# Storing the last group's output as two half tiles from two queues, in a fused attention and gated feed-forward kernel

## The chip, the cores and the metric

The kernel runs on one core of a Trainium2 chip. The core has a matrix engine (TensorE, PE in the rows; its weight loads are PEld), a vector engine (VectorE, DVE), an activation engine (ScalarE, ACT), GpSimd (POOL) and SyncE (SP), which here does nothing but issue transfers and wait. Transfers are carried by 16 DMA engines that all issuing engines share; each issuer has a queue of its own, in the rows q1 for SyncE, q10 for ScalarE and q0 for GpSimd. The metric is the device time of one execution in microseconds (us). The times are medians of several executions.

## The reference

Two branches read the same x of 2048 tokens by 512: attention with 32 heads of size 16 that share one k and one v, and a GeGLU feed-forward layer of width 1376. A sigmoid gate for each token mixes them. All is float32.

```python
def _A_ref(x, wq, wk, wv, wo):
    q = (x @ wq).reshape(B, S, H, Dh).transpose(0, 2, 1, 3)
    k = x @ wk
    v = x @ wv
    scores = einsum("bhqd,bkd->bhqk", q, k) * (Dh ** -0.5)
    o = einsum("bhqk,bkd->bhqd", softmax(scores), v)
    return o.transpose(0, 2, 1, 3).reshape(B, S, H * Dh) @ wo

def _B_ref(x, w_gate, w_up, w_down):
    return (gelu(x @ w_gate) * (x @ w_up)) @ w_down

g = sigmoid((x * gate_w).sum(-1, keepdims=True))
return g * _A_ref(...) + (1 - g) * _B_ref(...)
```

## The kernel before

The 2048 tokens are four groups of 512 (`NTG`, `TG`). The operands of the projections and of the feed-forward layer are split in a high and a low half, and each product is done in three passes. After a prologue, a table of lines (`PLAN`) sets the order on TensorE by hand: each line plays one job of the feed-forward layer (`f`) or of the output projection (`w`), with score matmuls and value matmuls of the attention put between its pieces.

For each group an accumulator `acc[g]` of 128 x 4 x 512 in SBUF holds four row tiles of 128 tokens. The feed-forward jobs add to it, weighted by one minus the gate (line 617). Then, for each row tile i, the output projection's matmuls leave a bank in PSUM, and `wo_out` (lines 625 to 628) adds that bank, times the gate, to the row tile with one VectorE instruction (line 627) and stores the finished 128 x 512 tile, 256 KB, to `out` with one transfer that SyncE issues (line 628).

Groups 0 to 2 reach `wo_out` through jobs of the table, in the middle of the stream. The last group, 3, is done behind the table (lines 882 to 889): twelve chains of matmuls first sum up three quarters of the projection for all four row tiles, while VectorE finishes the last heads' normalisation (lines 776 to 794); then, row tile by row tile, three matmuls end the chain (line 501) and `wo_out` follows. No other work comes after it. ScalarE's last work is the last exponential of the scores (line 749).

Each engine runs its own instructions in the order in which they are written, and semaphores tie them to each other. Transfers issued by SyncE or ScalarE count on eight semaphores, DMAHW0 to DMAHW7, which the transfers of the whole program take in turn. At the end of the program (rows of line 928) SyncE waits for all of them, in the order of their numbers and each in an instruction of its own, before all engines meet and the program is over.

Of the kernel before, what the change touches and what calls it, by code (L numbers as in the profile page):

```python
# [19 lines left out]
P = 128  # L20
# [5 lines left out]
TG = 512  # L26
NTG = S // TG
# [84 lines left out]
def mix_kernel(ctx, tc, xT, wq, wo, wf, out):  # L112
    nc = tc.nc
# [511 lines left out]
    def wo_out(g, i, ps):  # L625
        o = acc[g][:, i]
        nc.vector.scalar_tensor_tensor(o, ps, gt[:, 4 * g + i : 4 * g + i + 1], o, op0=ALU.mult, op1=ALU.add)  # L627
        nc.sync.dma_start(out[g * TG + i * P : g * TG + (i + 1) * P], o)

    def wo_job(g, i):  # L630
        def begin():
            assert ("o", 0, NB - 1) in done
            flush(bg)
            return [[t for bl in range(NB) for t in wo_terms(g, k, bl)] for k in (i, i + 1)]

        def end(z, y):
            wo_out(g, i, z)
            wo_out(g, i + 1, y)

        return begin, end  # L640
# [44 lines left out]
    with tc.If(v > 0):  # L685
        with tc.tile_pool(name="gp", bufs=1) as gp:
# [4 lines left out]
            with tc.For_i(0, NTG * NB, 1) as gb:  # L691
                with tc.For_i(0, 2, 1) as a:
                    t = gp.tile([P, 2, TG], F32R, tag="gq", name="gq", bufs=2)
                    rows = scr[bass.ds(gb, 1)].rearrange("o r (a h) q -> (o r) a h q", a=2)
# [187 lines left out]
    g = NTG - 1  # L882
# [4 lines left out]
    for i, ps in enumerate(tail):  # L887
        chain_mm(ps, wo_terms(g, i, NB - 1), first=False)
        wo_out(g, i, ps)
# [42 lines left out]
```

## Time and profile before

| what | us |
|---|---|
| median of 3 runs | 1230.28 |
| range of the runs | 1230.28 to 1230.36 |
| the profiled execution, its own time | 1231.25 |
| its span, first to last instruction | 1229.5 |
| TensorE busy in the span | 1222.6 |
| ScalarE busy in the span | 1029.4 |
| VectorE busy in the span | 546.1 |

The profile is one execution, taken by the hardware's profiler. A row of the timeline has the start in us from the span's start, the length, the engine, the line of the kernel, the operation, what it writes and reads, and how many instructions the row merges. An engine's name with a q behind it is its sequencer, which waits, branches and issues transfers: a row "SPq ... DMA_DIRECT2D" is the time in which SyncE issues, not the time in which the bytes move. When they move is told by the DMA view and by the windows, whose last two columns are the mean busy share of the 16 DMA engines and the GB/s that they moved. A share a little over 1 arises where a packet that began in a window ends after it.

### The profile page before, as it was taken

The page shows a single profiled execution, that of the slowest core. Times are in us where ns is not written, and L with a number is a line of the kernel's source. Part 1 is how long each engine was busy: PE and PEld are TensorE (multiplying, and loading weights), DVE is VectorE, ACT ScalarE, POOL GpSimd, SP SyncE. Part 2 cuts the span into 40 slices and gives each one's busy share as a digit, 9 for nine tenths or more (in the row PEclk, how much of TensorE's full clock was granted, in tenths as well). Part 3 has the DMA queues.
Part 4 walks back from the last instruction along what each step waited for, and adds up shares of the span by engine and source line. Part 5 has one row for each costly group of instructions (what it writes and reads, how often), then busy time and mean ns, then how long its engine had stood idle before and what let it go on. Part 6 is the DMA issues. An engine that isn't in the chain of part 4 may idle for free.

```text
span 1229.5 us, 23232 instructions
## 1 busy us (share of the span) xinstructions
PE 1222.6 (99%) x9742; PEld 671.4 (55%) x9742; DVE 546.1 (44%) x812; ACT 1029.4 (84%) x1127; POOL 216.9 (18%) x188
## 2 busy tenths in 40 slices
PE   9999999999999999999999999999999999999998
PEld 6875455555554555455555555654554555545545
DVE  7774422656245151545436152263626244044624
ACT  5549888888888888998888888889888898889983
POOL 5422201222121010212112020121311011012100
PEclk9999999999999999999999999999999999999999
DMA  8641202212021110122211120111211211002000
GB/s 333 211 135 52 72 1 58 66 53 79 27 68 51 44 32 23 49 57 67 66 35 58 39 76 15 42 44 56 83 41 49 75 49 32 23 27 66 15 1 35
DMA packets 39835, 73.88 MB, mean 60 GB/s; under 512 B 5488, under 2 KB 5744, under 8 KB 39728
## 3 DMA queue, kind: packets, MB, share of 16 engines
q1 hardware_dynamic: 39184, 71.32, 18.9%
q8 instruction: 77, 1.26, 0.4%
q0 software_dynamic: 256, 0.79, 0.2%
q14 instruction: 30, 0.25, 0.1%
q10 hardware_dynamic: 288, 0.26, 0.1%
HBM read 57.41 MB, written 14.94 MB: 59 GB/s over the span
## 4 chain that ended last, share of the span: by engine, by line
PE 93%; DVE 0%; ACT 0%; issue 0%
PE acc L816 38%; PE s L745 23%; PE z L515 21%; PE y L515 10%; PE wos L501 1%; PE u L501 0%; DVE acc L627 0%; ACT p L749 0%; PE wof L501 0%; DVE sq L545 0%; DVE sq L544 0%; DVE gs L541 0%; ACT sq L548 0%
## 5 line engine op out<-in xcount | busy, mean ns | idle before, releaser
L749 ACT ACTIVATE p<-s 128x1024 f32<-128x1024 f32 x1024 | 976.3, 1026 | 139.1 <-PE s L745 136.2
L816 PE MATMUL acc<-p,v 128*32 128x512 f32 x4096 | 484.8, 597 | 0.0
L745 PE MATMUL s<-Q,kp 51*128 51x512 f32 x2048 | 384.8, 415 | 0.1
L745 PEld LDWEIGHTS s<-Q,kp 51*128 51x128 f32 x2048 | 184.2, 184 | 214.1 <-ACT p L749 124.0
L816 PEld LDWEIGHTS acc<-p,v 128*32 128x32 f32 x4096 | 114.3, 109 | 250.8 <-issue 242.1
L187 POOL TENSOR_TENSOR gl<-st,gh 128x512 fp32r<-128x512 f32 x80 | 114.0, 1444 | 754.3 <-PE s L745 375.5
L515 PE MATMUL z<-xh,gh 64*128 64x512 f32 x312 | 125.9, 403 | 0.0
L515 PE MATMUL y<-xh,gh 64*128 64x512 f32 x312 | 125.8, 403 | 0.0
L515 PE MATMUL y<-xl,gh 64*128 64x512 f32 x312 | 122.4, 392 | 0.0
L515 PE MATMUL z<-xl,gh 64*128 64x512 f32 x312 | 122.1, 391 | 0.0
L515 PE MATMUL z<-xh,gl 64*128 64x512 f32 x312 | 121.8, 390 | 0.0
L515 PE MATMUL y<-xh,gl 64*128 64x512 f32 x312 | 121.7, 390 | 0.0
L541 DVE COPY gs<-z 128x512 f32<-128x512 f32 x39 | 27.0, 692 | 195.3 <-PE y L515 128.5
L187 POOL TENSOR_TENSOR dl<-st,dh 128x512 fp32r<-128x512 f32 x44 | 57.3, 1304 | 127.8 <-PE s L745 94.0
L515 PE MATMUL z<-dh,hh 64*128 64x512 f32 x176 | 69.5, 395 | 0.0
L515 PE MATMUL y<-dh,hh 64*128 64x512 f32 x176 | 69.5, 395 | 0.0
L515 PE MATMUL y<-dl,hh 64*128 64x512 f32 x176 | 68.9, 392 | 0.0
L515 PE MATMUL z<-dl,hh 64*128 64x512 f32 x176 | 68.8, 391 | 0.0
L515 PE MATMUL z<-dh,hl 64*128 64x512 f32 x176 | 68.8, 391 | 0.0
L515 PE MATMUL y<-dh,hl 64*128 64x512 f32 x176 | 68.7, 391 | 0.0
L515 PEld LDWEIGHTS z<-xh,gh 64*128 64x128 f32 x312 | 58.0, 186 | 15.6 <-POOLq L523 7.3
L515 PEld LDWEIGHTS z<-xl,gh 64*128 64x128 f32 x312 | 58.3, 187 | 8.2
(173 smaller groups left out, 1458.0 us busy)
## 6 DMA issues: line engine op xcount, KB each, us to landing
st<-wf SPq DMA_DIRECT2D x125, 256.0 KB
scr<-q SPq DMA_DIRECT2D x16, 512.0 KB
Q<-scr SPq DMA_DIRECT2D x64, 128.0 KB
Q<-scr SPq DMA_DIRECT2D x64, 64.0 KB
out<-acc SPq DMA_DIRECT2D x16, 256.0 KB
xr<-xT SPq DMA_DIRECT2D x6, 512.0 KB
st<-xT SPq DMA_DIRECT2D x12, 256.0 KB
xr<-xT SPq DMA_DIRECT2D x4, 256.0 KB
```

The costliest lines, as they stand in the source:

```text
L187: eng_l.tensor_sub(lo, src, hi)
L501: nc.tensor.matmul(ps, a, b, start=(first and q == 0), stop=(last and q == len(terms) - 1), skip_group_check=True)
L515: mm = nc.tensor.matmul(ps, a[rs], b[rs], start=(half == 0 and q == 0), stop=(half == 1 and q == len(X) - 1), skip_group_check=True)
L541: nc.vector.tensor_copy(gs, g)
L745: nc.tensor.matmul(ps[:, j * TG : (j + 1) * TG], kp[rs, kc * P : (kc + 1) * P], Q[u][rs, pr], start=True, stop=True)
L749: nc.scalar.activation(pb[s][:, pr], ps, AF.Exp, bias=0.0, scale=SCALE)
L816: nc.tensor.matmul(accp[u][32 * j : 32 * j + 32], vt[:, kc], pb[s][:, j // 2, (j % 2) * TG : (j % 2 + 1) * TG], start=(kc == 0), stop=(kc ...
```

## The change

`wo_out` keeps its VectorE instruction. For groups 0 to 2 the store is as before. For the last group each store is written as two: rows 0 to 63 of the tile from SyncE, rows 64 to 127 from ScalarE. Each half is 128 KB.

```diff
     def wo_out(g, i, ps):
         o = acc[g][:, i]
         nc.vector.scalar_tensor_tensor(o, ps, gt[:, 4 * g + i : 4 * g + i + 1], o, op0=ALU.mult, op1=ALU.add)
-        nc.sync.dma_start(out[g * TG + i * P : g * TG + (i + 1) * P], o)
+        rows = out[g * TG + i * P : g * TG + (i + 1) * P]
+        if g < NTG - 1:
+            nc.sync.dma_start(rows, o)
+        else:
+            nc.sync.dma_start(rows[0 : P // 2], o[0 : P // 2])
+            nc.scalar.dma_start(rows[P // 2 : P], o[P // 2 : P])
```

The last instructions of SyncE before the change, from the last loads of the attention's queries (`Q`) on; `acc` is the accumulator of the last group, and behind "waits" stand the semaphores that an instruction waits for:

```order
L368 DMA Q_12177<-scr 16x2x512
L373 DMA Q_12177<-shs 3x2x512 [waits DMAHW2_49]
L373 DMA Q_12177<-shs 3x2x512 [waits DMAHW3_49]
L628 DMA out<-acc_11092 128x512 [waits DMAHW4_49,DVE_49]
L628 DMA out<-acc_11092 128x512 [waits DMAHW5_49,DVE_49]
L628 DMA out<-acc_11092 128x512 [waits DMAHW6_49,DVE_49]
L628 DMA out<-acc_11092 128x512 [waits DMAHW7_49,DVE_49]
L928 UNCONDITIONAL_BRANCH
```

Each store takes the next semaphore; it waits until the earlier transfer that counted on the same semaphore is over, and for VectorE. The same place after the change, on SyncE:

```order
L368 DMA Q_12177<-scr 16x2x512
L373 DMA Q_12177<-shs 3x2x512 [waits DMAHW2_49]
L373 DMA Q_12177<-shs 3x2x512 [waits DMAHW3_49]
L632 DMA out<-acc_11092 64x512 [waits DMAHW5_49,DVE_49]
L632 DMA out<-acc_11092 64x512 [waits DMAHW7_49,DVE_49]
L632 DMA out<-acc_11092 64x512 [waits DMAHW1_49,DVE_49]
L632 DMA out<-acc_11092 64x512 [waits DMAHW3_49,DVE_49]
L933 UNCONDITIONAL_BRANCH
```

and at the end of ScalarE, where before the change the branch followed the last exponential:

```order
L754 ACTIVATE p<-s 128x1024 [waits PE_49]
L633 DMA out<-acc_11092 64x512 [waits DMAHW4_49,DVE_49]
L633 DMA out<-acc_11092 64x512 [waits DMAHW6_49,DVE_49]
L633 DMA out<-acc_11092 64x512 [waits DMAHW0_49,DVE_49]
L633 DMA out<-acc_11092 64x512 [waits DMAHW2_49,DVE_49]
L933 UNCONDITIONAL_BRANCH
```

SyncE still issues four times, each for half the rows; ScalarE has four issues more; and the last pair of stores counts on DMAHW2 and DMAHW3, where the last store counted on DMAHW7. The order on the other engines is the same.

## The prediction

> **What bounds the kernel now.** I read the page first, then the chain of waits over the end of the span, then the timeline and the DMA view of that end, because the change touches nothing before it. The page:
>
> ```profile
> span 1229.5 us, 23232 instructions
> PE 1222.6 (99%) x9742; PEld 671.4 (55%) x9742; DVE 546.1 (44%) x812; ACT 1029.4 (84%) x1127; POOL 216.9 (18%) x188
> ```
>
> TensorE is busy in 99% of the span, so the time is TensorE's stream plus what follows its last matmul. The stores of groups 0 to 2 lie under that stream and are not changed. The chain of waits, from 1222 us on (start, length, what), the timeline there, and TensorE's, VectorE's and SyncE's rows:
>
> ```profile
> 1222.20 0.69 PE wos L501 x3
> 1222.90 0.02 issue
> 1222.92 2.79 DVE acc L627 x4
> ...
> 1210.79 1.03 ACT L749 ACTIVATE p<-s 128x1024 f32<-128x1024 f32 x1
> ...
> 1224.53 0.39 PE L501 MATMUL wof<-woh,ol 128*128 128x512 f32 x1
> 1224.96 0.75 DVE L627 SCALAR_TENSOR_TENSOR acc<-wof,gt,acc 128x512 f32<-128x512 f32 x1
> ...
> 1223.70 2.37 SPq L628 DMA_DIRECT2D out<-acc  x4
> ```
>
> The chain ends with four additions of VectorE, each worth about 0.7 us, the last over at 1222.92 + 2.79 = 1225.71. SyncE issues one store behind each of them, from 1223.70 to 1226.07. ScalarE's last exponential is over at 1211.82, so ScalarE is idle here. From 1225.71 to the end of the span, 1229.5, there is no arithmetic: 3.8 us of stores and closing. That is the whole stage this change can act on. The DMA engines in it, by windows (columns: stretch, length, busy time of PE, PEld, DVE, ACT, POOL, clock, DMA share, GB/s):
>
> ```profile
> 1223.60:1224.50 0.90, 0.90 (x5) 0.75 (x4) 0.90 (x3) 0.00 (x0) 0.00 (x0) 1.00 0.00 0
> 1224.57:1227.46 2.90, 0.35 (x2) 0.00 (x0) 1.14 (x2) 0.00 (x0) 0.00 (x0) 1.00 0.96 362
> 1224.57:1225.25 0.68, 0.35 (x2) 0.00 (x0) 0.68 (x2) 0.00 (x0) 0.00 (x0) 1.00 0.98 364
> 1225.25:1227.30 2.05, 0.00 (x0) 0.00 (x0) 0.46 (x1) 0.00 (x0) 0.00 (x0) 1.00 1.02 384
> 1227.46:1229.49 2.03, 0.00 (x0) 0.00 (x0) 0.00 (x0) 0.00 (x0) 0.00 (x0) 0.55 0.02 4
> ```
>
> Nothing moves for 0.87 us after the first issue (1223.70 to 1224.57). Then the 16 engines are full until 1227.46, at 362 GB/s: four stores of 256 KB are 1.05 MB, and 1.05 / 0.362 = 2.9 us. The stores come one each 0.68 us and one takes 0.256 / 0.38 = 0.68 us to move, so the engines never run dry and never fall far behind. Two things therefore set the end of the transfers at the same place: the first byte plus 2.9 us of bytes (1227.46), and the last store by itself, which if it met empty engines would end at 1225.74 + 0.87 + 0.68 = 1227.3. Behind the bytes SyncE's own waits are the last to end:
>
> ```profile
> SPq L928 <- DMA out<-acc: 1.2, 2, 0.6
> ...
> L928 SPq EVENT_SEMAPHORE  x8: 17/28/28, 1226.1 to 1226.5; - x8
> ...
> L928 SPq EVENT_SEMAPHORE  x2: 28/28/28, 1227.2 to 1227.8; - x2
> L928 SPq DRAIN  x1: 7/7/7, 1227.9 to 1227.9; - x1
> ```
>
> The ten closing waits of SyncE are in these rows: the first eight find their semaphores ready and start 0.4 / 7 = 0.06 us apart; the ninth runs at 1227.2 and the tenth at 1227.8, each held back by a store. The tenth waits for the last store, and runs 0.36 us after the last byte. Then come a drain and the meeting of all engines, to 1229.5.
>
> **The change, part by part.**
>
> *Issue.* Four stores of 128 rows on SyncE become four of 64 rows there and four of 64 rows on ScalarE. What is queued behind them: on SyncE only the closing waits, on ScalarE only its closing branch. One issue costs, by the rows of SyncE over the whole kernel (ns, least / median / most):
>
> ```profile
> L628 SPq DMA_DIRECT2D out<-acc x16: 332/353/375, 407.1 to 1225.7; - x16
> ...
> L367 SPq DMA_DIRECT2D Q<-scr x64: 312/414/1487, 70.6 to 1140.7; - x64
> L368 SPq DMA_DIRECT2D Q<-scr x64: 414/425/1307, 71.1 to 1141.2; - x64
> ```
>
> Line 628 issues 128 runs of 2 KB, line 367 issues 64, line 368 issues 32. Fewer runs are not cheaper: 0.35, 0.41, 0.43 us. So a half costs SyncE 0.33 to 0.43 us, ends before the next store is due 0.68 us later, and I take 0 change. Nor does the delay to the first byte hang on the size. A lone 64-run load and a lone 128-run load:
>
> ```profile
> 1139.89 0.33 SPq L367 DMA_DIRECT2D Q<-scr  x1
> ...
> 1139.80:1140.80 1.00, 1.00 (x14) 0.33 (x12) 0.96 (x2) 0.90 (x1) 0.00 (x0) 1.00 0.00 0
> 1140.80:1140.90 0.10, 0.10 (x8) 0.03 (x2) 0.10 (x1) 0.10 (x2) 0.00 (x0) 1.00 0.91 123
> ...
> 1131.57 0.33 SPq L349 DMA_DIRECT2D st<-wf  x1
> ...
> 1131.50:1132.50 1.00, 1.00 (x12) 0.83 (x10) 0.00 (x0) 1.00 (x2) 0.04 (x1) 1.00 0.00 0
> 1132.50:1132.60 0.10, 0.10 (x4) 0.08 (x2) 0.00 (x0) 0.10 (x1) 0.00 (x0) 1.00 0.49 123
> ```
>
> Both start to move between 0.91 and 1.03 us after their issue. So SyncE's first half should move at 1224.57, as now. For ScalarE's half the only row is the program's start, where both queues issue at once:
>
> ```profile
> 0.76 0.40 ACTq L166 DMA_DIRECT2D st<-wf  x1
> ...
> 0.77 1.83 SPq L169 DMA_DIRECT2D xr<-xT  x4
> ...
> q1 hardware_dynamic: 8, 0.02, 13.4%
> ...
> q1 hardware_dynamic: 33, 0.07, 71.8%
> q10 hardware_dynamic: 33, 0.02, 16.3%
> ```
>
> The third row is the DMA view of 1.80 to 2.25 us, where only SyncE's queue (q1) moves; the last two are 2.25 to 2.60 us, where ScalarE's (q10) has joined. Issued together, ScalarE's first byte came about 0.44 us after SyncE's. The delay of ScalarE's half is so bounded by 0.87 and 0.87 + 0.44 us. At the first it costs nothing. At the second, ScalarE's first half moves at 1225.01 while SyncE's 128 KB last until 1224.57 + 0.34 = 1224.91: the engines lose 0.1 us once. I take the nearer end, 0, and keep 0.1 for the range.
>
> *Bytes.* The same 1.05 MB move on the same 16 engines, with 16 more of the smallest packets for each of the four added transfers:
>
> ```profile
> DMA packets 576, 1.05 MB, mean 328 GB/s; under 512 B 64, under 2 KB 64, under 8 KB 576
> ```
>
> Of 576 packets 64 are under 512 B, 16 a store; now they will be 128. Were one as long as a mean packet (0.96 x 2.90 x 16 / 576 = 0.077 us), the added four on each engine would cost 0.31 us. But the stretch that holds nearly all of them ran at 384 GB/s and the stretch that holds none at 364, so they cost next to nothing: I take 0.03, with 0 and 0.31 for the range.
>
> [...]
>
> *The closing waits.* Each transfer counts on the next of eight semaphores in turn, and SyncE closes by waiting for them by number, DMAHW0 to DMAHW7. The order of instructions shown ahead has the last stores before on DMAHW4 to 7, so the last to land was the last waited for. After the change they run over 4, 5, 6, 7, 0, 1, 2, 3, and the last pair, 2 and 3, lands while SyncE has five or four more waits to walk. At 0.06 us each, that is 0.24 to 0.3 us which lie under the transfers now and will lie behind the last byte. I take 0.3. It would be 0 if the waits' cost ran beside the 0.36 us that a landing takes to be seen, and that is the lower end.
>
> *Sum.* Issue 0, bytes 0.03, closing waits 0.3: +0.33 us. The profiled execution has 1231.25 us, 1229.5 of span and 1.75 around it, so its like after the change has 1231.6 with a span of 1229.8. The median of the plain runs is 1230.28, 0.97 below that execution; the same step on it gives 1230.6.
>
> **The rivals.** First, *the issue hardware serves the two queues in turn*. For it speaks the 0.44 us at the start; against it that SyncE's issues there were no longer than alone. If every half took 0.44 us, the eighth would begin at 1224.57 + 7 x 0.44 = 1227.65 and end 0.34 later, at 1227.99: 0.53 us late, and with the closing waits 1230.28 + 0.53 + 0.3 = 1231.1.
>
> Second, *two queues fill the engines better*. For it a row of the busiest stretch, 20.0 to 20.5 us, where two queues share the engines:
>
> ```profile
> DMA packets 86, 0.21 MB, mean 426 GB/s; under 512 B 15, under 2 KB 15, under 8 KB 86
> ...
> q0 software_dynamic: 39, 0.11, 56.9%
> q1 hardware_dynamic: 47, 0.10, 50.6%
> ```
>
> At 426 GB/s the last store still begins at 1225.74 + 0.87 and ends 0.6 later, 1227.21: a gain of 0.25 against +0.3 of waits, 1230.2. Against it: the engines are already full at a share of 1.02. Were the waits free besides, it would be 1230.0, and that is the best case I can build. A gain of 0.2% would have to end the transfers before VectorE's last addition.
>
> Third, on the other side, *half the rows, half the rate*: 64 rows can be read only half as fast, and both queues' packets come in step, so that the engines ask first for the upper rows and then for the lower. At half of 362 GB/s the transfers take 5.8 us instead of 2.9; with the waits 1230.28 + 2.9 + 0.3 = 1233.5, 0.26% slower. It decides from a mean rate under about 210 GB/s (2.9 + 2.16 us), where the 2.46 us of 0.2% are reached. Against it is the same row: q0 there is GpSimd's store of 32 rows (786 KB in all from a zeroed tile),
>
> ```profile
> shs<-woh POOLq DMA_DIRECT2D x4, 192.0 KB, 7.1
> ```
>
> and it moved 0.11 MB in 0.5 us, 220 GB/s, beside another queue's 0.10 MB, with the engines' total at 426. A quarter of the rows did not slow the engines, so two interleaved halves should not.
>
> That the change does not do what it says can be excluded on the issue side: the order of instructions has the four halves on ScalarE, behind its last exponential, with nothing else there.
>
> **How the numbers follow.** Forecast 74%; served in turn 10%; better filled 8%; half the rate 6%; and 2% for shifts that I cannot name. About 0.2%, 2.46 us, is what a measurement of this kernel can tell from no change. Only the third rival passes it: slower 6%, faster 1%, the same 93%. The predicted time is the forecast's, 1230.6. The range takes in the first two rivals and the added bounds (0.1 for ScalarE's delay, 0.31 for small packets): 1230.1 to 1231.4; below and above it lie the half-rate case and the far ends, less than 2 in 10.
>
> **What would show it.** Right: q1 and q10 with about 0.52 MB each in the last 5 us, together at 360 to 390 GB/s from 1224.6 to 1227.5; four ACTq issues of 0.33 to 0.47 us from 1223.7 on; four or five closing waits of SyncE 0.06 us apart after 1227.5, and a span longer by 0.3. Wrong: q10's first byte more than 0.5 us behind q1's, gaps in the DMA row, a rate near 200 GB/s, or a closing that follows the last byte as fast as now. Any change of TensorE's stream before 1222 us would also make the sum wrong, since I give it none.

## The result and the profile after

| | before | after |
|---|---|---|
| median of 14 executions, us | 1230.32 | 1232.66 |
| lowest and highest, us | 1229.93, 1231.39 | 1232.02, 1233.41 |
| profiled execution: time, span, us | 1231.25, 1229.5 | 1233.26, 1231.5 |

The ratio after to before is 1.0017, with a 95% interval of [1.0009, 1.0025]: 2.1 us longer, between 1.1 and 3.1 (the two medians are 2.3 apart). The forecast was 0.33 us longer, 1230.6, and the stated range ended at 1231.4. Executions of one kernel differ by over a microsecond, and the profiles differ by as much in their first 80 us, far ahead of the edited stores: the first exponential starts at 81.3 us in the profile of before, at 81.5 after, at 79.6 and 79.9 in two of the runs below. So the parts are measured here from the end of VectorE's last addition, behind which only the stores and the closing lie. Before, that tail lasts from 1225.71 to 1229.49: 3.78 us.

The timeline after the change, VectorE's and the two issuing queues' rows (start, length, engine, line, operation):

```profile
1223.22 2.11 DVE L627 SCALAR_TENSOR_TENSOR acc<-wos,gt,acc 128x512 f32<-128x512 f32 x3 [0.58 <-PE wos L501]
1225.26 0.75 DVE L627 SCALAR_TENSOR_TENSOR acc<-wof,gt,acc 128x512 f32<-128x512 f32 x1
...
1224.00 2.78 SPq L632 DMA_DIRECT2D out<-acc  x4
1224.01 2.51 ACTq L633 DMA_DIRECT2D out<-acc  x4
```

The last addition ends at 1226.01, 0.30 later than in the profile of before, and the tail is 1231.46 - 1226.01 = 5.45 us: 1.67 us longer. The two sum to the 1.97 us by which the span grew. The windows of the tail (stretch, length, busy times, clock, DMA share, GB/s), and the issues in ns (least / median / most):

```profile
1223.90:1225.20 1.30, 1.30 (x6) 0.75 (x4) 1.30 (x3) 0.00 (x0) 0.00 (x0) 1.00 0.00 0
1225.20:1225.80 0.60, 0.02 (x1) 0.00 (x0) 0.60 (x2) 0.00 (x0) 0.00 (x0) 1.00 0.98 201
1225.80:1226.40 0.60, 0.00 (x0) 0.00 (x0) 0.21 (x1) 0.00 (x0) 0.00 (x0) 1.00 0.99 362
1225.80:1229.06 3.26, 0.00 (x0) 0.00 (x0) 0.21 (x1) 0.00 (x0) 0.00 (x0) 1.00 0.84 285
1225.20:1229.06 3.86, 0.02 (x1) 0.00 (x0) 0.81 (x2) 0.00 (x0) 0.00 (x0) 1.00 0.86 272
1229.06:1231.46 2.40, 0.00 (x0) 0.00 (x0) 0.00 (x0) 0.00 (x0) 0.00 (x0) 0.65 0.01 3
...
L633 ACTq DMA_DIRECT2D out<-acc x4: 474/490/545, 1224.0 to 1226.0; - x4
...
L632 SPq DMA_DIRECT2D out<-acc x4: 546/580/782, 1224.0 to 1226.2; - x4
```

Three places grew. The first byte comes 1225.20 - 1224.00 = 1.20 us after the first issue, where it came after 0.87: +0.33. The bytes take 3.86 us instead of 2.89: +0.97. From the last byte to the end of the span it is 2.40 instead of 2.03: +0.37. That is 1.67 us, the whole of the longer tail.

How slow a packet is follows from the share and the rate: share x 16 engines x 2048 B / rate is the mean engine time of 2 KB. Before it was 0.96 x 16 x 2048 / 362 = 87 ns. In the first 0.6 us after the change it is 0.98 x 16 x 2048 / 201 = 160 ns: the engines are full and move little more than half as much. In that time only ScalarE's queue moves (DMA view, 1225.00 to 1225.81, then to 1229.1):

```profile
q10 hardware_dynamic: 61, 0.12, 73.7%
...
q1 hardware_dynamic: 320, 0.52, 48.6%
q10 hardware_dynamic: 259, 0.40, 34.6%
```

So the engines first move ScalarE's rows 64 to 127 alone, at little more than half the rate, and SyncE's half, issued at the same moment, does not move until that one is nearly through. SyncE's half then moves fast: from 1225.80 to 1226.40 us the rate is 362 GB/s, 90 ns for 2 KB, and the DMA view of 1226.0 to 1226.2 us has 0.08 MB of SyncE's queue there at a share of 98.7%, and next to nothing of ScalarE's. A half is therefore not slow every time that it moves alone; why this one was not, no run shows. From 1225.80 us on, a packet costs 0.84 x 16 x 2048 / 285 = 97 ns on the mean, with idle time between (share 0.84). Of the 0.97 us, longer packets are 0.86 x 3.86 - 0.96 x 2.90 = 0.54, and engines that stood idle are the rest.

SyncE's closing waits, from 1229.1 to 1229.85 us:

```profile
L933 SPq EVENT_SEMAPHORE  x6: 28/28/28, 1229.3 to 1229.8; - x6
```

Six closing waits run after the last byte, where before it was the last one only.

### The profile page after: what moved, and what is told of

It reads as the page before. It is cut to its first block, busy times and chain, and to the rows that moved or that the text cites. A ratio compares the mean times of both kernels' runs of the same rounds, so it can differ in the third digit from the quotient of the medians.

```text
span 1231.5 us, 23240 instructions
## 1 busy us (share of the span) xinstructions
PE 1222.7 (99%) x9742; PEld 669.6 (54%) x9742; DVE 546.1 (44%) x812; ACT 1029.7 (84%) x1127; POOL 217.0 (18%) x188
## 4 chain that ended last, share of the span: by engine, by line
PE 93%; DVE 0%; ACT 0%; issue 0%
PE acc L821 38%; PE s L750 23%; PE z L515 22%; PE y L515 8%; PE wos L501 1%; PE u L501 0%; DVE acc L627 0%; ACT p L754 0%; PE wof L501 0%; DVE sq L544 0%; DVE sq L545 0%; DVE gs L541 0%; ACT sq L548 0%
## 5 line engine op out<-in xcount | busy, mean ns | idle before, releaser
L515 PEld LDWEIGHTS z<-xh,gl 64*128 64x128 f32 x312 | 57.6, 185 | 10.3
```

The source lines that it names most:

```text
L515: mm = nc.tensor.matmul(ps, a[rs], b[rs], start=(half == 0 and q == 0), stop=(half == 1 and q == len(X) - 1), skip_group_check=True)
```

## The experiments

Two theories were set against each other for the bytes. **A (rows):** one half of the tile's rows alone can be read only at about half the rate, so it is the choice of rows that costs. **B (two queues):** the two issuers, meeting at once, slow each other's issues and leave gaps. The edits are to the changed kernel's two lines for the last group's halves, except in the last pair of runs. In what follows the windows of the bytes begin with the first packet and end with the last.

### Both halves from SyncE

```diff
-            nc.scalar.dma_start(rows[P // 2 : P], o[P // 2 : P])
+            nc.sync.dma_start(rows[P // 2 : P], o[P // 2 : P])
```

> Both halves of each of the last four stores (rows 0 to 63, rows 64 to 127) are issued by SyncE, none by ScalarE; the halves are those of the changed kernel. Theory A (rows): all engines read one half of the rows at a time, so packets take about 150 to 165 ns instead of 84 while they do, as in the changed kernel's first 0.6 us at 201 GB/s, whatever queue issued them; the transfers take 3.5 to 5 us, and mean packet length over the stretch is well above 84 ns. Theory B (two queues at once): the slow issues (0.55 to 0.78 us on SyncE) and the gaps come from the two issuers meeting; with one issuer each issue is back to 0.33 to 0.43 us, packets take 84 ns, first byte 0.87 us after the first issue. By B the eighth issue starts about 7 x 0.47 = 3.3 us after the first, so the bytes end about 0.75 us later than before for that reason alone. Time: A +1.5 to +2.5 us against the kernel before, B about +1.0.

Measured: 1232.99 us, ratio to before 1.0027 [1.0017, 1.0037]. The issues, and the windows of the bytes and of what follows:

```profile
L632 SPq DMA_DIRECT2D out<-acc x4: 540/542/577, 1222.5 to 1226.4; - x4
L633 SPq DMA_DIRECT2D out<-acc x4: 590/595/603, 1223.1 to 1227.0; - x4
...
1223.74:1228.98 5.24, 0.00 (x0) 0.00 (x0) 0.79 (x2) 0.00 (x0) 0.00 (x0) 0.82 0.90 200
1228.98:1231.22 2.24, 0.00 (x0) 0.00 (x0) 0.00 (x0) 0.00 (x0) 0.00 (x0) 0.50 0.01 4
```

One queue alone is slower than two: 5.24 us at 200 GB/s, with 0.90 x 16 x 2048 / 200 = 147 ns for 2 KB. The packets are as slow as theory A has them, but the stretch is longer than its 3.5 to 5 us, and the tail, 6.69 us, is 2.91 over before where A had at most 2.5. That length is not the packets' alone. SyncE's eight issues follow one another, the first at 1222.51 and the eighth at 1226.97 us, one each 0.64 us, and 128 KB each 0.64 us are 206 GB/s. Even had the last half come 1.23 us after its issue, like the first, and then moved in 0.34 us, the bytes would have ended at about 1228.5 (an estimate from these rows). So some 1.9 of the 2.35 us over before are the issues, and only the length of the packets speaks for the rows. Theory B falls as the cause for the slow packets, and for the long issue too: one issuer alone spends 0.54 to 0.60 us on a half.

### Even rows from SyncE, odd rows from ScalarE

```diff
-            nc.sync.dma_start(rows[0 : P // 2], o[0 : P // 2])
-            nc.scalar.dma_start(rows[P // 2 : P], o[P // 2 : P])
+            nc.sync.dma_start(rows[0:P:2], o[0:P:2])
+            nc.scalar.dma_start(rows[1:P:2], o[1:P:2])
```

> Two queues and two transfers of 64 rows as in the changed kernel, but SyncE stores the even rows and ScalarE the odd ones, so each transfer touches rows all over the tile. Theory A (rows): the packets are back to 84 ns from the first byte on, the rate to 360 to 390 GB/s, the stretch of bytes to 2.9 to 3.1 us; what is left over the kernel before is the later first byte and 0.3 of closing waits, +0.3 to +0.8 us. Theory B (two queues): nothing changes against the changed kernel: issues of 0.5 to 0.8 us, second queue's first byte 0.6 us behind the first's, 272 GB/s over the stretch, +1.8 us.

Measured: 1230.98 us, ratio 1.0006 [0.9996, 1.0016]. The issues, and the windows:

```profile
L632 SPq DMA_DIRECT2D out<-acc x4: 553/588/787, 1223.9 to 1226.2; - x4
L633 ACTq DMA_DIRECT2D out<-acc x4: 478/504/556, 1223.9 to 1226.0; - x4
...
1225.15:1228.07 2.92, 0.01 (x1) 0.00 (x0) 0.80 (x2) 0.00 (x0) 0.00 (x0) 1.00 0.98 359
1228.07:1230.42 2.35, 0.00 (x0) 0.00 (x0) 0.00 (x0) 0.00 (x0) 0.00 (x0) 0.95 0.01 3
```

The same two queues, counts of rows and eight transfers, but other rows: the packets are back at 0.98 x 16 x 2048 / 359 = 89 ns and the bytes at 2.92 us (before 2.89). 0.94 of the 0.97 us lost on the bytes is due to which rows form a half. The issues stay long, the first byte stays 1.21 us after the first issue (1223.94), and 2.35 us remain behind the last byte: the tail is 4.47 us, 0.69 over before. So the other two parts are not due to which rows are taken.

### Rows 0 to 63 alone, even rows alone, rows 32 to 95 alone

Each of these issues from SyncE only, in place of the two halves. They store part of the output and ran once each, so only their rows are read, not their times:

```diff
+            nc.sync.dma_start(rows[0 : P // 2], o[0 : P // 2])   # first run
+            nc.sync.dma_start(rows[0:P:2], o[0:P:2])             # second run
+            nc.sync.dma_start(rows[32:96], o[32:96])             # third run
```

> Only rows 0 to 63 of the last group's four tiles are stored, by SyncE; rows 64 to 127 of them are left out, so half the bytes move. Theory A (rows): each 128 KB takes about 0.64 us at 200 GB/s with packets of 150 to 165 ns, the engines are busy nearly all of 2.6 us for half the bytes, and the end comes as late as with whole stores. Theory B: 84 ns packets, each 128 KB in 0.34 us, the engines idle half of the time, last byte about 1.2 us after the last issue.

> Only the even rows of the last group's four tiles are stored, by SyncE; the odd rows are left out. Beside the run that stored rows 0 to 63 alone (193 GB/s, each 128 KB in about 0.64 us) it changes only which 64 rows. Theory A (rows): 84 to 88 ns packets, each 128 KB in 0.34 us, the engines idle half of the time, last byte about 1.6 us after the last issue or sooner instead of 1.9. If 64 rows are slow wherever they lie: as in the run of rows 0 to 63. Issue: 0.47 to 0.58 us and the first byte 1.2 us after it if the count of rows sets it, 0.33 to 0.37 and 0.87 if their place does.

> Only rows 32 to 95 of the last group's four tiles are stored, by SyncE; the other rows are left out. 64 neighbouring rows as in the run of rows 0 to 63, but across the middle of the tile. If what slows is that all engines read the same half of the partitions (0 to 63), these rows lie on both sides and move at 84 to 88 ns a packet, 128 KB in 0.34 us. If 64 neighbouring rows are slow wherever they lie, the packets take 145 to 160 ns again. Issue 0.47 to 0.59 us and first byte 1.2 us after it in either case.

The windows of the bytes, one row for each run in this order, and for the even rows also the first 0.34 us:

```profile
1224.94:1227.66 2.72, 0.00 (x1) 0.00 (x0) 0.79 (x2) 0.00 (x0) 0.00 (x0) 0.87 0.88 193
...
1223.85:1226.27 2.42, 0.00 (x0) 0.00 (x0) 0.78 (x2) 0.00 (x0) 0.00 (x0) 1.00 0.58 217
1223.85:1224.19 0.34, 0.00 (x0) 0.00 (x0) 0.34 (x2) 0.00 (x0) 0.00 (x0) 1.00 0.94 355
...
1224.19:1226.63 2.44, 0.00 (x0) 0.00 (x0) 0.72 (x2) 0.00 (x0) 0.00 (x0) 1.00 0.58 215
```

Each moves 0.52 MB. Rows 0 to 63 keep the engines at a share of 0.88 for it: 149 ns for 2 KB. Even rows, and neighbouring rows that lie across the middle of the tile, take 88 ns and leave the engines idle for 42% of the stretch. The length of a stretch says little here, since the stores come 0.68 us apart in all three. It is therefore not 64 rows, nor neighbouring rows, but rows of one side of the 128 partitions, 0 to 63 here and 64 to 127 at the start of the changed kernel's stores, that take 149 to 160 ns instead of 87; SyncE's first half after the change, at 90, is the exception that stays unexplained. One thing stays joined to it in every run: a row of the tile also has its place in `out`, so rows of one side fill one half of a tile's 256 KB there, while even rows and rows 32 to 95 reach both halves. Whether the reading of the tile or the writing of `out` is slow, these runs do not separate.

### Thirty-two and ninety-six rows

```diff
+            nc.sync.dma_start(rows[0:32], o[0:32])   # first run
+            nc.sync.dma_start(rows[0:96], o[0:96])   # second run
```

> Only rows 0 to 31 are stored, by SyncE, a quarter of the bytes; the other rows are left out. Rows: packets of 145 to 160 ns, as for rows 0 to 63, since they lie on the same side. Issue: if it grows as the count of rows falls below 128, 0.6 us or more; if 64 rows were a case of their own, 0.33 to 0.43.

> Only rows 0 to 95 are stored, by SyncE, three quarters of the bytes; rows 96 to 127 are left out. Two thirds of the rows lie on one side, one third on the other: packets between 84 and 150 ns on the mean, about 110. Issue: between those of 128 rows (0.33 to 0.37 us) and of 64 rows (0.47 to 0.59 us) if the count sets it.

The bytes of the two runs, then the issues of five runs: 32 rows, 96 rows, and rows 0 to 63, even rows, rows 32 to 95:

```profile
1223.49:1225.92 2.43, 0.37 (x2) 0.00 (x0) 1.16 (x2) 0.00 (x0) 0.00 (x0) 1.00 0.45 107
...
1223.33:1226.64 3.31, 0.36 (x2) 0.00 (x0) 1.15 (x2) 0.00 (x0) 0.00 (x0) 1.00 0.76 236
...
L632 SPq DMA_DIRECT2D out<-acc x4: 315/323/354, 1222.6 to 1224.7; - x4
...
L632 SPq DMA_DIRECT2D out<-acc x4: 316/324/356, 1222.5 to 1224.5; - x4
...
L632 SPq DMA_DIRECT2D out<-acc x4: 467/508/577, 1223.7 to 1225.8; - x4
...
L632 SPq DMA_DIRECT2D out<-acc x4: 472/516/587, 1222.6 to 1224.7; - x4
...
L632 SPq DMA_DIRECT2D out<-acc x4: 542/558/642, 1222.9 to 1224.9; - x4
```

The bytes came near to what theory A has: 138 ns for 2 KB from 32 rows of one side (0.45 x 16 x 2048 / 107), beside 149 from 64, and 105 ns for 96 rows, two thirds of which lie on one side. Three quarters of the bytes took 3.31 us, longer than all of them in whole stores. The issue did not go as either reading had it. It does not grow as the rows get fewer: 32 and 96 rows cost 0.32 to 0.36 us, like 128, with the first byte 0.85 and 0.86 us after the issue. Of these five, only the three runs with 64 rows pay 0.47 to 0.64 us, with the first byte 1.22 to 1.29 us after it. Why 64 is a case of its own these runs do not show.

### Halves by columns

```diff
-            nc.sync.dma_start(rows[0 : P // 2], o[0 : P // 2])
-            nc.scalar.dma_start(rows[P // 2 : P], o[P // 2 : P])
+            nc.sync.dma_start(rows[:, 0 : D // 2], o[:, 0 : D // 2])
+            nc.scalar.dma_start(rows[:, D // 2 : D], o[:, D // 2 : D])
```

> Each of the last four stores as two halves by columns: all 128 rows, 256 columns each (128 runs of 1 KB, 128 KB), one from SyncE and one from ScalarE. It keeps the two queues and the eight transfers, and gives each transfer all rows. Theory A (rows), as it stands after the even-and-odd run: bytes at 360 to 385 GB/s in 2.9 us. On the issue there are two readings: if 64 rows make the issue long (0.47 to 0.58 us, first byte 1.2 us after), it is back to 0.33 to 0.40 us and 0.87 us here, and only the closing waits of 0.35 us are left over the kernel before, +0.3 to +0.5 us; if the meeting of two queues makes it long, it stays at 0.5 to 0.6 us, +0.6 to +0.9 us. Theory B (two queues): 270 GB/s, +1.8 us.

Measured: 1231.03 us, ratio 1.0006 [0.9996, 1.0015]. Issues and windows:

```profile
L632 SPq DMA_DIRECT2D out<-acc x4: 332/347/376, 1222.9 to 1224.9; - x4
L633 ACTq DMA_DIRECT2D out<-acc x4: 365/374/383, 1222.9 to 1224.9; - x4
...
1223.77:1226.99 3.22, 0.34 (x2) 0.00 (x0) 1.13 (x2) 0.00 (x0) 0.00 (x0) 0.98 0.99 325
1226.99:1229.37 2.38, 0.00 (x0) 0.00 (x0) 0.00 (x0) 0.00 (x0) 0.00 (x0) 0.50 0.01 3
```

With 128 rows in each transfer both queues issue in 0.33 to 0.38 us though they do it at the same moment, and the first byte is back at 0.88 us. The meeting of the queues costs the issue next to nothing; it is the 64 rows that put off the first byte by 0.33 us. The bytes were expected at 2.9 us and took 3.22, with full engines: 100 ns for 2 KB in runs of 1 KB instead of 87 in runs of 2 KB. So the tail is 4.47 us, 0.69 over before, where 0.3 to 0.5 were expected. The 2.38 us behind the last byte stay, as expected with the eight transfers in the same order.

### Whole stores, alternating

```diff
-            nc.sync.dma_start(rows[0 : P // 2], o[0 : P // 2])
-            nc.scalar.dma_start(rows[P // 2 : P], o[P // 2 : P])
+            (nc.sync, nc.scalar)[i % 2].dma_start(rows, o)
```

> Whole 128-row stores, tiles 0 and 2 issued by SyncE, 1 and 3 by ScalarE: two queues, no halves, issues 0.68 us apart. Theory A: as before the change, 360 to 385 GB/s, time within 0.3 us of before. Theory B: also as before, since the issues no longer meet; only if ScalarE's queue is slow in itself would its stores start more than 0.9 us after their issue, and the time be longer by that.

Measured: 1229.92 us, ratio 1.0001 [0.9991, 1.0010]: no difference that can be told.

```profile
1222.91:1225.82 2.91, 0.36 (x2) 0.00 (x0) 1.15 (x2) 0.00 (x0) 0.00 (x0) 1.00 0.97 360
1225.82:1227.42 1.60, 0.00 (x0) 0.00 (x0) 0.00 (x0) 0.00 (x0) 0.00 (x0) 1.00 0.00 0
```

Issue (0.35 to 0.37 us on either queue) and bytes (360 GB/s) are those of before; ScalarE's queue is not slow in itself. Behind the last byte there are 1.60 us instead of 2.03, so that this is the shortest tail of all kernels with the full output, 3.36 us. Within the measurement it does not beat the kernel before. The next runs tell where the 0.43 us come from.

### Four small loads more, to move the semaphores

Put ahead of the last group's output, in the changed kernel and in the kernel before:

```diff
+    pad = cp.tile([1, 16], F32, name="pad")
+    for k in range(4):
+        nc.sync.dma_start(pad[:, 4 * k : 4 * k + 4], wq[0:1, 0, 4 * k : 4 * k + 4])
     g = NTG - 1
```

> The changed kernel with four loads of 16 bytes more on SyncE, issued some 80 us before the last stores. They move the stores by four semaphores, so that the last pair counts on DMAHW6 and DMAHW7, the last that SyncE waits for. If the walk over the remaining closing waits lies behind the last byte, the time from the last byte to the end of the span falls from 2.40 to about 2.03 us, and the time by 0.3 us against the changed kernel; if something else made that end long, it stays at 2.4 us. The bytes are unchanged, 270 GB/s.

> The kernel before with the same four small loads: whole stores, but the last one counts on DMAHW3, with four closing waits behind it. If those waits cost 0.06 to 0.07 us each, the time from the last byte to the end of the span rises from 2.03 to about 2.3 us and the time by 0.3 us; if they are hidden, it stays. Bytes and issues as before.

The windows behind the last byte, of the changed kernel with the loads and of the kernel before with them:

```profile
1230.63:1232.27 1.64, 0.00 (x0) 0.00 (x0) 0.00 (x0) 0.00 (x0) 0.00 (x0) 0.50 0.02 5
...
1227.62:1229.87 2.25, 0.00 (x0) 0.00 (x0) 0.00 (x0) 0.00 (x0) 0.00 (x0) 1.00 0.01 4
```

With the last store waited for in the middle, the closing of the kernel before rises from 2.03 to 2.25 us, about as the walk over the closing waits has it (2.3 was expected). With the last pair waited for last, the closing of the changed kernel falls from 2.40 to 1.64, by more than the 0.37 that were looked for. The surplus is a second thing, a step in SyncE's own instructions: before and after the change, the drain that follows its last wait and the next one begin 0.4 us apart, and in the changed kernel with the loads, as with the whole stores alternating, they do not. The rows of the drains in these four:

```profile
L928 SPq DRAIN  x2: 7/63/119, 1227.9 to 1228.3; - x2
...
L933 SPq DRAIN  x2: 7/62/117, 1229.9 to 1230.2; - x2
...
L936 SPq DRAIN  x2: 7/7/7, 1231.1 to 1231.2; - x2
...
L932 SPq DRAIN  x2: 7/7/7, 1226.3 to 1226.3; - x2
```

In the kernel before with the loads the step lies earlier, between two closing waits behind the last store, 1228.1 and 1228.5 us (two windows, 1227.95 to 1228.20 and 1228.20 to 1228.65):

```profile
L931 SPq EVENT_SEMAPHORE  x2: 28/28/28, 1228.0 to 1228.1; - x2
...
L931 SPq EVENT_SEMAPHORE  x3: 28/28/28, 1228.5 to 1228.6; - x3
```

So the closings add up: without walk and step 1.60 to 1.64 us, with the step alone 2.03, with the step and a walk 2.25 and 2.40. The step is in the kernels before and after alike, and the difference between them is the walk.

The times did not follow. The changed kernel with the loads took 1232.81 us (ratio to before 1.0020 [1.0010, 1.0029]), so the 0.3 us expected against the changed kernel, 1232.66, are not there, though its tail is 4.59 us, 0.86 shorter. The kernel before with the loads took 1231.90 us (1.0014 [1.0004, 1.0024]), though its tail is only 3.96 us, 0.18 longer. The remaining difference, more than 1 us, is not in the tail. Part of it is in TensorE's stream: TensorE is busy for 1224.4 and 1223.5 us with the loads, where it is 1222.7 and 1222.6 without. The edit also puts a tile more into the first pool. Why TensorE takes longer stays open, so these two runs count only for what their rows show of the closing.

## Why the prediction was wrong

**The frame held.** TensorE's stream did not change (1222.6 and 1222.7 us busy); the whole difference that belongs to the change is in the tail, and its three parts are those that the sum had: issue, bytes, closing waits.

Two of the sum's steps failed: that a half of 64 rows is issued and started like a whole store, and that its bytes move at the same rate.

**"Issue 0" failed, by 0.33 us.** It was argued from line 367, whose loads have 64 runs and cost 0.33 to 0.41 us. Those are 32 rows with two runs each. The stores of the change have 64 rows of one run; they cost 0.47 to 0.78 us and put off the first byte by 0.33, and 32, 96 and 128 rows did not. Why is open. The nearest row shared the number of runs but not the shape.

**"Bytes 0.03" failed, and it is the larger miss: 0.97 us.** For what it priced, the small packets of four more transfers, 0.03 fits: with even and odd rows the bytes take 2.92 us instead of 2.89. What the sum put at nothing is which rows make a half, and that is the other 0.94. The mechanism was named, as the third rival, with a chance of 6% and a price of 2.9 us. The row used against it was misread. GpSimd's store from 32 rows moved 220 GB/s while the engines' total was 426, and that was taken as proof that few rows do not slow a transfer. But 220 is about what one side gives with full engines (an estimate: 193 GB/s at a share of 0.88 and 200 at 0.90 in the runs above make 219 and 222 at a share of 1), and the other queue filled the rest. Nor does the row prove the rival: its packets, 0.569 x 16 x 500 ns for 0.11 MB, took 85 ns for 2 KB, the fast ones. It could not decide, since a total over two queues says nothing on one transfer's limit. The rival itself was too hard, since it let the halves stay slow to the end: the stores began as it has them, the upper rows alone at 201 GB/s, but later ran at 285, and lost 0.97 us instead of 2.9.

**"Closing waits 0.3" was right,** as a size and as a mechanism: 0.37 us in the trace, and 0.32, 0.35 and 0.21 in the three other runs with eight transfers in that order (2.35, 2.38 and 2.24 us). The loads that moved the semaphores moved the walk with them; the step of 0.4 us, which they also took away, is no part of the difference.

**"ScalarE's delay 0 to 0.44 us"** was near: by columns, ScalarE's first packets came in the window up to 1223.92 us and not in that up to 1223.88, so 0.11 to 0.15 us after SyncE's at 1223.77. In the changed kernel it was SyncE's half that came later, 0.61 us after ScalarE's (1225.20 to 1225.81), about as long as ScalarE's first half moved.

**The first rival, served in turn,** was nearer in its price (1231.1) than the forecast, but that is luck. The first two halves of the changed kernel did begin one behind the other, yet with even and odd rows the engines stayed full all the same (share 0.98, bytes 0.03 us longer), and by columns the two queues issued together at 0.33 to 0.38 us (share 0.99). **The second, better filled engines,** did not come: no run with the full output moved its bytes faster than the 362 GB/s of before. (Its price is also mis-added in the prediction: 1230.28 - 0.25 + 0.3 is 1230.3, not 1230.2.)

The chance of 93% for no difference above 0.2% rested on these two failed steps. The measured 0.17% lies below that bound, with an interval that reaches over it; that it does is luck, since the tail grew by 1.67 us where 0.33 were forecast.

## What to carry to other kernels

Split a store so that each part still takes rows of both sides of the 128 partitions: whole tiles, and even and odd rows, kept the rate here (360 and 359 GB/s), halves at row 64 did not (272); by columns the shorter runs of 1 KB had their own price (325). With the engines already full (share 0.96), a second queue gave nothing (ratio 1.0001), and a last transfer that counted on a semaphore waited for early left a walk behind the last byte, 0.2 to 0.4 us. When a row is used against a rival, compare its rate with the rate that the rival itself would give there.

## What was unexpected of the hardware

Stores of 64 rows on SyncE took 0.47 to 0.64 us to issue (up to 0.79 with ScalarE issuing beside it), and the first byte came 1.20 to 1.29 us after the first issue started, in every run with such stores, whichever 64 rows they took; stores of 32, 96 or 128 rows took 0.32 to 0.38 us, and their first byte came after 0.85 to 0.88. In SyncE's closing there is a step of some 0.4 us that was not in the same place in every run: between two drains before and after the change (1227.9 to 1228.3, 1229.9 to 1230.2), between two waits in the kernel before with four loads more (1228.1 to 1228.5). What it is was not tried.
